# A second, shifted copy of exp(K) gives one of three small AV units its own PE row tiles

## The chip, the core and the metric

The kernel runs on one core of a Trainium2 chip. The metric is the device time of one execution in microseconds (us). Most executions of one kernel agree within 0.3%, so a gain of 1 us (0.3%) needs several rounds, or the trace, to be seen. Ratios are the mean time of one kernel's runs over that of the other's of the same rounds, so not quite the ratio of the medians that are quoted.

## The reference, cut to what matters

Local plus global attention (8 batches, 8 heads, 512 local and 32 global positions, head dimension 64), followed by a feed-forward block with a quick GELU. What the change touches is the part of the local queries that looks at the 32 global keys:

```python
s_lg = scale * np.matmul(q_l, k_g.transpose(0, 1, 3, 2))      # 512 x 32 for each head
s_l = np.concatenate([s_lg, s_ll], axis=-1)                   # beside the window of local keys
out_l = np.matmul(sm(s_l), np.concatenate([v_g, v_l], axis=2))
```

## The kernel before

Four heads make a "quad" and are worked on together; there are 16 quads. `K` computes the global-key scores of a quad into one PSUM bank (a section of the memory that matmuls write) `kb`, in two halves of the head dimension (`e` = 0, 1), each four matmuls with 32 rows and 32 columns of the PE array. `XK` takes the exponential: `ek`. `ekU` (the AV units of the title: attention weights times values) multiplies it with one of three stationary operands (unit 0: ones, for the sums; units 1 and 2: the two halves of the global values), and `U` adds the local keys to the same three banks with all 128 rows.

```python
def gk(self, out_, rhs, e=None):              # K(e): rows 32j, columns 32((j+1)%4)
    for ee in (0, 1) if e is None else (e,):
        for j in range(4):
            p = slice(32 * j, 32 * j + 32)
            r = 32 * ((j + 1) % 4)
            nc.tensor.matmul(out_[r : r + 32], lhsT=self.kg[p, :, ee], rhs=..., ...)

def ekU(self, unit, warm=0, ov=None):         # rows 32((j+1)%4), columns 32j, for every unit
    ...
    for j in range(4):
        r = 32 * ((j + 1) % 4)
        p = slice(r, r + 32)
        lv = (ones32[p] if unit == 0 else
              rvg[p, self.Q, :D].rearrange("p (w h) -> p w h", h=2)[:, :, unit - 1])
        nc.tensor.matmul(ov[32 * j : 32 * j + 32, :], lhsT=lv, rhs=self.ek[p], start=True, ...)

def ekUs(self, nxt=None, rnd=0, banks=(None, None, None)):
    if nxt:
        if rnd is not None:
            nxt.gg(rnd)                       # 8 matmuls of 32 columns, on K's tiles
        nxt.K(0)                              # the NEXT quad's scores, first half
    self.ekU(0, ov=banks[0])
    if nxt:
        nxt.K(1)                              # second half
    self.ekU(1, ov=banks[1])
    self.ekU(2, ov=banks[2])
```

In this kernel a matmul's rows of the array are those of its operands' partitions and its columns those of its output's partitions. All heads of `ek` stand at 32((j+1) mod 4), so all three units share four array tiles.

The softmax here doesn't subtract the row's maximum and nothing guards it: scores larger than these inputs give would overflow.

Of the kernel before, what the change touches and what calls it, by code (L numbers as in the profile page):

```python
# [13 lines left out]
BF16 = mybir.dt.bfloat16  # L14
# [6 lines left out]
def kernel(  # L21
# [12 lines left out]
    nc = tc.nc  # L34

    B, H, Sl, D = q_l.shape
# [8 lines left out]
    NQ = B * 2  # L45
# [9 lines left out]
    consts = ctx.enter_context(tc.tile_pool(name="consts", bufs=1))  # L55
    wts = ctx.enter_context(tc.tile_pool(name="wts", bufs=1))
    ld = ctx.enter_context(tc.tile_pool(name="ld", bufs=3))
    att = ctx.enter_context(tc.tile_pool(name="att", bufs=2))
# [14 lines left out]
    def load(b, us=(0, 1), kq=True):  # L73
        if b not in loaded:
            loaded[b] = (ld.tile([128, 2, 16 * D], BF16, name="rk"),
                         ld.tile([128, 2, 16 * D], BF16, name="rq"))
        if kq:
            s = slice(us[0], us[-1] + 1)
            nc.gpsimd.dma_start(out=loaded[b][1][:, s], in_=qf[b][:, s])
            nc.gpsimd.dma_start(out=loaded[b][0][:, s], in_=kf[b][:, s])  # L80
# [3 lines left out]
    def load_v(b, us=(0, 1)):  # L84
        s = slice(us[0], us[-1] + 1)
        hs = slice(4 * us[0], 4 * us[-1] + 4)
        for g in range(4):
            p = slice(32 * g, 32 * g + 32)
            nc.gpsimd.dma_start(out=vtiles[b % 2][p, s, :, :, :D], in_=vf[b, g][:, hs])  # L89
# [2 lines left out]
    rkg = consts.tile([128, NQ, D], BF16)  # L92

    rvg = consts.tile([128, NQ, D + 2], BF16)

    def load_turned(eng, out_, in_):
        eng.dma_start(out=out_[32:128], in_=in_[0:96])
        eng.dma_start(out=out_[0:32], in_=in_[96:128])

    def load_g(lo, hi):  # L100
        nc.gpsimd.dma_start(out=rkg[:, lo:hi, :], in_=kgf[:, lo:hi, :])
        nc.gpsimd.dma_start(out=rqg[:, lo:hi, :], in_=qgf[:, lo:hi, :])
        load_turned(nc.gpsimd, rvg[:, lo:hi, :D], vgf[:, lo:hi, :])
# [33 lines left out]
    for j in range(4):  # L137
        r = (j + 1) % 4
# [19 lines left out]
    def keep(n, ps, w=512):  # L158
        for _ in range(n):
            nc.tensor.matmul(ps[:, :w], lhsT=warm[:, 0:128], rhs=warm[:, :w], start=True, stop=True)  # L160
# [35 lines left out]
    def transpose_g(lo, hi, names="qk"):  # L196
        for name, dst, s in (("q", qgT, rqg), ("k", kgT, rkg)):
            if name not in names:
                continue
            nc.vector.transpose(dst[:, lo:hi, :32], s[:, lo:hi].bitcast(F32))  # L200
# [29 lines left out]
    def pbank(name):  # L230
        return psP.tile([128, 512], F32, name=name, tag="p")

    class Quad:
# [123 lines left out]
            self.gr = rnd  # L357
            self.gk((self.ps if rnd else self.spt(0))[:, 2, RW : RW + 32], self.qg)

        def XK(self):  # L360
            self.ek = att.tile([128, Sl], BF16, name="ek")
            nc.scalar.activation(self.ek, self.kb, AF.Exp, scale=scale)  # L362

        def ekU(self, unit, warm=0, ov=None):
            if ov is None:
                ov = pbank("ov")
            self.st[unit] = ov
            keep(warm, ov)
            for j in range(4):
                r = 32 * ((j + 1) % 4)  # L370
                p = slice(r, r + 32)
                lv = (ones32[p] if unit == 0 else
                      rvg[p, self.Q, :D].rearrange("p (w h) -> p w h", h=2)[:, :, unit - 1])
                nc.tensor.matmul(ov[32 * j : 32 * j + 32, :], lhsT=lv, rhs=self.ek[p],  # L374
                                 start=True, stop=False, skip_group_check=True)

        def ekUs(self, nxt=None, rnd=0, banks=(None, None, None)):
            if nxt:
                if rnd is not None:
                    nxt.gg(rnd)  # L380
                nxt.K(0)
            self.ekU(0, ov=banks[0])
            if nxt:
                nxt.K(1)
            self.ekU(1, ov=banks[1])
            self.ekU(2, ov=banks[2])

        def U(self, unit):
# [95 lines left out]
    def o_mm(i, st):  # L484
        tci, f4 = divmod(st, 4)
        first = (i, tci) not in ops
        if first:
            ops[i, tci] = pbank("op")
        op = ops[i, tci]
        for fc in range(4 * f4, 4 * f4 + 4):  # L490
            nc.tensor.matmul(op, lhsT=gTs[i][:, fc, tci * 128 : tci * 128 + 128],  # L491
                             rhs=w_out_sb[:, fc, :], start=(first and fc == 4 * f4), stop=(fc == FC - 1))
        if f4 == 3:
            o_out(i, tci, op)
# [27 lines left out]
    a, c = Quad(0), Quad(1)  # L522
# [35 lines left out]
    cast_g32("v", rvg)  # L558
    c.B(0)
    a.K()  # L560
    a.XK()
    c.S(0, added=True)
    c.gg()
    c.X(0)
    a.eg()
    c.K()
    c.XK()
    a.ekU(0)
    a.U(0)
    a.R()  # L570
# [51 lines left out]
    a, c = nq[1]  # L622
# [5 lines left out]
    a.gg()  # L628
    a.K()
    a.X(0)  # L630
    a.XK()
    a.M(0)
    a.eg()
    c.T()
# [10 lines left out]
    c.S(1)  # L645
    a.ekUs(c, 1)
    c.X(1)
    c.XK()
    for unit in range(3):
        a.U(unit)  # L650
    a.R()
# [20 lines left out]
    a, c = nq[2]  # L672
    load_v(3)
    load(4)
    load_g(8, NQ)
    gTs[1] = moe.tile([128, FC, TB], BF16, name="gT")
    hps = [pbank("hp") for _ in range(2)]
    for fc, kcs in ((0, (0, 1)), (1, (0, 1)), (0, (2, 3)), (1, (2, 3))):
# [20 lines left out]
    def phase_o(i):  # L699
        b = i + 1  # L700
        n = b + 1
        a, c = nq[b]
        if n < B:
            nq[n] = (Quad(2 * n), Quad(2 * n + 1))
            a2, c2 = nq[n]

        def o(tci):
            for f4 in range(4):
                o_mm(i, 4 * tci + f4)

        c.T()
        c.ext()
        a.S(1)
        a.X(1)
        a.M(1)
        o(0)
        c.S(0)
        a.UG(c)
        c.XK()
        c.X(0)  # L720
        a.RXG()
        c.M(0)
        c.eg()
        o(1)
        if n < B:
            a2.T()
            transpose_g(2 * n, 2 * n + 2)
            a2.ext()
        c.S(1)
        c.X(1)  # L730
        c.M(1)
        if n < B:
            o(2)
            a2.S(0)
            c.UG(a2)
            a2.XK()
            a2.X(0)
        else:
            for f4 in range(3):
                o_mm(i, 8 + f4)  # L740
            for unit in range(3):
                c.ekU(unit)
                c.U(unit)
            o_mm(i, 11)
            c.Gm()
        c.RXG()
        if n < B:
            a2.M(0)
            a2.eg()
        o(3)  # L750
        if i + 3 < B:
            load_v(i + 3)
        if i + 4 < B:
            load(i + 4)

    for i in range(1, B):
        if i > 1:
            for fc in range(FC):
                h_step(i, fc)
        if i + 1 < B:  # L760
            phase_o(i)
# [36 lines left out]
```

## Time and profile before

| | before |
|---|---|
| median (lowest to highest), first 3 runs | 311.05 us (310.76 to 311.09) |
| span of the profiled run | 309.3 us |
| PE busy, share of the span | 299.2 us, 97% |
| the stage from the first unit to the local products | 0.75 to 0.76 us, 11 times |

The prediction below shows the lines. PE is the matmul engine and PEld its weight loads; DVE, ACT and POOL are the vector, scalar and general engines; SP here only issues DMAs, as its queue SPq. The page gives busy times of each engine; "the chain that ended last" follows the last instruction back to what released it. In a timeline the columns are start, duration (both us), engine, line of the kernel, operation, output and inputs, shapes and count. Durations of matmuls overlap: what counts is when the next group starts.

### The profile page before, as it was taken

What the parts mean: (1) busy time and instruction counts of PE and PEld (TensorE: products, weight loads), DVE (VectorE), ACT (ScalarE), POOL (GpSimd) and SP (SyncE); (2) the same over time, 40 slices, a digit from 0 to 9 for tenths busy, and PEclk for the clock granted to TensorE, in tenths of its full rate; (3) what the DMA queues carried; (4) which work ended last, traced back from release to release, by engine and by line L of the source; (5) the groups of instructions that cost most, each with busy time, mean ns of one, the idle gap of its engine ahead of it and who ended that gap; (6) DMA issues with size and microseconds to landing.
All of it is one profiled execution on the core that took longest, in us unless ns stands there. A gap on an engine that the chain in (4) does not pass through costs nothing.

```text
span 309.3 us, 7765 instructions
## 1 busy us (share of the span) xinstructions
PE 299.2 (97%) x3230; PEld 149.3 (48%) x3265; DVE 211.0 (68%) x446; ACT 167.6 (54%) x251; POOL 54.1 (18%) x86
## 2 busy tenths in 40 slices
PE   7899999999999999999999999999999999999994
PEld 6544445444454455444454455445454454446653
DVE  6668857978957876776867876776777855573320
ACT  4728475475546735565556645565456651673421
POOL 8542754630050001400050002100000000000000
PEclk9999999999999999999999999999999999999999
DMA  7999999999289013951199013901120012201122
GB/s 193 176 209 206 201 138 217 213 184 100 61 79 192 5 36 72 131 107 30 45 95 173 8 37 71 101 0 36 36 61 10 2 44 46 51 0 35 35 68 69
DMA packets 53859, 27.60 MB, mean 89 GB/s; under 512 B 42432, under 2 KB 43712, under 8 KB 53824
## 3 DMA queue, kind: packets, MB, share of 16 engines
q0 software_dynamic: 45696, 16.95, 48.2%
q1 hardware_dynamic: 7648, 9.51, 12.6%
q10 hardware_dynamic: 480, 0.66, 0.7%
q8 instruction: 25, 0.41, 0.6%
q14 instruction: 10, 0.08, 0.1%
HBM read 35.13 MB, written 8.91 MB: 142 GB/s over the span
## 4 chain that ended last, share of the span: by engine, by line
PE 88%; DVE 4%; ACT 2%; DMA 2%; issue 1%; POOL 1%; ACTq 0%; POOLq 0%
PE op L491 35%; PE hp L466 35%; PE s L297 6%; PE ov L397 4%; PE ov L374 3%; DMA rk<-in_k_l_dram 2%; ACT e L327 1%; DVE xL L430 1%; PE s L316 1%; PE op L503 1%; DVE gT L474 1%; PE s L466 1%; PE s L415 1%; ACT th L473 1%; PE kb L316 1%
## 5 line engine op out<-in xcount | busy, mean ns | idle before, releaser
L491 PE MATMUL op<-w_out_sb,gT 128*128 128x512 bf16 x504 | 120.0, 380 | 1.7 <-issue 0.5
L474 DVE SCALAR_TENSOR_TENSOR gT<-th,hp 128x512 bf16<-128x512 f32 (+1 forms) x140 | 91.1, 656 | 41.8 <-ACT th L473 40.5
L466 PE MATMUL hp<-xL,w_in_sb 128*128 128x512 bf16 x487 | 108.4, 379 | 0.7
L473 ACT ACTIVATE th<-hp 128x512 f32<-128x512 f32 (+1 forms) x140 | 79.8, 573 | 42.9 <-PE hp L466 39.4
L466 PEld LDWEIGHTS <-w_in_sb 128*128 128x128 bf16 x576 | 56.1, 98 | 65.0 <-issue 1.3
L491 PEld LDWEIGHTS <-gT 128*128 128x128 bf16 x528 | 49.3, 98 | 56.4 <-issue 3.5
L327 ACT ACTIVATE e<-s 128x1712 bf16<-128x1712 f32 x31 | 49.5, 1597 | 15.8 <-PE s L415 8.9
L505 ACT ACTIVATE ob<-op 128x512 f32<-128x512 f32 (+2 forms) x35 | 20.5, 585 | 60.3 <-PE op L491 57.7
L89 POOL DMA_DIRECT2D v<-in_v_l_dram x24 | 18.7, 786 | 115.9 <-PE s L415 111.0
L421 DVE STREAM_TRANSPOSE sT<-ov 128x512 f32<-128x512 f32 x15 | 10.8, 717 | 29.1 <-PE ov L397 29.1
L334 DVE TENSOR_TENSOR e<-e,mask 128x1408 bf16<-128x1408 bf16 x28 | 24.4, 871 | 6.5 <-ACT e L327 6.5
L297 PE MATMUL s<-q,kT 32*128 32x228 bf16 (+5 forms) x528 | 21.1, 280 | 0.9 <-DVE q L259 0.7
L430 DVE TENSOR_TENSOR xL<-ov,rs 128x512 bf16<-128x512 f32 x30 | 19.4, 686 | 1.8 <-PE ov L397 0.5
L297 PEld LDWEIGHTS <-kT 32*128 32x128 bf16 x528 | 11.1, 95 | 14.8 <-issue 9.4
L255 DVE STREAM_TRANSPOSE kT<-rk 128x512 f32<-128x512 f32 (+1 forms) x17 | 16.9, 993 | 1.4 <-DMA rk<-in_k_l_dram 1.3
L362 ACT ACTIVATE ek<-kb 128x512 bf16<-128x512 f32 x16 | 9.6, 601 | 9.5 <-PE kb L316 9.5
L397 PE MATMUL ov<-e,v 128*32 128x160 bf16 (+1 forms) x480 | 12.1, 239 | 0.0
L425 DVE STREAM_TRANSPOSE rs<-rT 128x512 f32<-128x512 f32 x16 | 11.4, 711 | 0.5
L259 DVE STREAM_TRANSPOSE q<-rq 128x512 f32<-128x512 f32 (+1 forms) x17 | 10.7, 634 | 0.0
L397 PEld LDWEIGHTS <-v 128*32 128x32 bf16 x512 | 10.0, 97 | 0.9 <-issue 0.9
L316 PE MATMUL kb<-q,kgT 32*32 32x512 bf16 x128 | 10.0, 386 | 0.0
L466 PE MATMUL hp<-xG,w_in_sb 128*128 128x256 bf16 x64 | 9.6, 273 | 0.1
(78 smaller groups left out, 165.9 us busy)
## 6 DMA issues: line engine op xcount, KB each, us to landing
out_dram<-ob SPq DMA_DIRECT2D x132, 64.0 KB, 1.7
v<-in_v_l_dram POOLq DMA_DIRECT2D x32, 128.0 KB, 6.5
rq<-in_q_l_dram POOLq DMA_DIRECT2D x6, 512.0 KB, 8.5
rk<-in_k_l_dram POOLq DMA_DIRECT2D x6, 512.0 KB, 10.4
w_out_sb<-in_moe_w_out_dram POOLq DMA_DIRECT2D x4, 512.0 KB, 11.3
w_in_sb<-in_moe_w_in_dram POOLq DMA_DIRECT2D x4, 256.0 KB, 10.2
w_in_sb<-in_moe_w_in_dram POOLq DMA_DIRECT2D x2, 512.0 KB, 12.5
rq<-in_q_l_dram POOLq DMA_DIRECT2D x3, 256.0 KB, 7.9
```

The lines of the kernel that those rows point to most:

```text
L89: nc.gpsimd.dma_start(out=vtiles[b % 2][p, s, :, :, :D], in_=vf[b, g][:, hs])
L255: nc.vector.transpose(self.kT.rearrange("p (r t) -> p t r", t=16)[:, lo:hi], loaded[self.b][0][:, self.u].bitcast(F32)[:, 32 * lo : 32 * hi])
L297: nc.tensor.matmul(ps[j][:, off : off + n], lhsT=self.k[p, 128 * c : 128 * c + 128, e], rhs=self.q[p, lo:hi, r0 : r0 + nr, e], start=(e == ...
L327: nc.scalar.activation(e[:, :, :RW], self.ps[:, :, :RW], AF.Exp, scale=scale)
L334: nc.vector.tensor_mul(e, e, mask[:, rnd : rnd + 1, :].to_broadcast([128, 4, LW]))
L397: nc.tensor.matmul(ov[32 * j : 32 * j + 32, :].rearrange("p (t r) -> p t r", t=16)[:, :, r0 : r0 + nr], lhsT=lv, rhs=self.E[c // 2][:, j, ...
L430: nc.vector.tensor_mul(self.x[:, 2 * self.u + h, :], self.st[1 + h], self.st["rs"])
L466: nc.tensor.matmul(hp[:, : width(i)], lhsT=w_in_c[:, fc // 8, kc, fc % 8 // 2, :, fc % 2], rhs=(xL[i] if i < B else xG)[:, kc, :], start=( ...
L473: nc.scalar.activation(th[:, :n], hp[:, :n], AF.Tanh, scale=0.851)
L474: nc.vector.scalar_tensor_tensor(gTs[i][:, fc, :n], in0=th[:, :n], scalar=1.0, in1=hp[:, :n], op0=ALU.add, op1=ALU.mult)
L491: nc.tensor.matmul(op, lhsT=gTs[i][:, fc, tci * 128 : tci * 128 + 128], rhs=w_out_sb[:, fc, :], start=(first and fc == 4 * f4), stop=(fc = ...
L505: nc.scalar.activation(ob[:, lo:hi], op[:, lo:hi], AF.Copy, scale=0.5)
```

## The change

The intent: make a copy `ek2` of `ek` turned by 32 partitions, by DMA, and likewise of the global values (`rvt` from `rvg`); let unit 1 use the copies, so that it lands on other array tiles than unit 0 and the two run at once. Only quads 4 to 15 use it.

```diff
-        def XK(self):
+        def XK(self, two=True):
             self.ek = att.tile([128, Sl], BF16, name="ek")
             nc.scalar.activation(self.ek, self.kb, AF.Exp, scale=scale)
+            self.ek2 = None
+            if two:
+                self.ek2 = att.tile([128, Sl], BF16, name="ek2")
+                load_turned(nc.sync, self.ek2, self.ek)
...
             for j in range(4):
-                r = 32 * ((j + 1) % 4)
+                two = unit == 1 and self.ek2 is not None
+                r = 32 * ((j + 1 + two) % 4)
...
             self.ekU(0, ov=banks[0])
+            if self.ek2 is not None:
+                self.ekU(1, ov=banks[1])
             if nxt:
                 nxt.K(1)
-            self.ekU(1, ov=banks[1])
+            if self.ek2 is None:
+                self.ekU(1, ov=banks[1])
             self.ekU(2, ov=banks[2])
...
+    load_turned(nc.sync, rvt[:, 4:8], rvg[:, 4:8])
...
+        if i == 1:
+            load_turned(nc.sync, rvt[:, 8:NQ], rvg[:, 8:NQ])
```

(The operands follow: `rvt` and `ek2` in place of `rvg` and `ek` where `two` holds. The first four quads call `XK(False)`.)

More of the change, by code (lines that the diff above doesn't have):

```diff
@@ L94 @@
     rvg = consts.tile([128, NQ, D + 2], BF16)
+    rvt = consts.tile([128, NQ, D + 2], BF16)
     def load_turned(eng, out_, in_):
@@ L369, in ekU @@
             for j in range(4):
-                r = 32 * ((j + 1) % 4)
+                two = unit == 1 and self.ek2 is not None
+                r = 32 * ((j + 1 + two) % 4)
                 p = slice(r, r + 32)
                 lv = (ones32[p] if unit == 0 else
-                      rvg[p, self.Q, :D].rearrange("p (w h) -> p w h", h=2)[:, :, unit - 1])
-                nc.tensor.matmul(ov[32 * j : 32 * j + 32, :], lhsT=lv, rhs=self.ek[p],
+                      (rvt if two else rvg)[p, self.Q, :D].rearrange("p (w h) -> p w h", h=2)[:, :, unit - 1])
+                nc.tensor.matmul(ov[32 * j : 32 * j + 32, :], lhsT=lv, rhs=(self.ek2 if two else self.ek)[p],
                                  start=True, stop=False, skip_group_check=True)
@@ L560 @@
     a.K()
-    a.XK()
+    a.XK(False)
     c.S(0, added=True)
@@ L566 @@
     c.K()
-    c.XK()
+    c.XK(False)
     a.ekU(0)
@@ L630 @@
     a.X(0)
-    a.XK()
+    a.XK(False)
     a.M(0)
@@ L647 @@
     c.X(1)
-    c.XK()
+    c.XK(False)
     for unit in range(3):
```

## The prediction

> **What bounds the kernel now.** I read the page first (busy shares, clock, the chain that ended last), then the chain in order of time to find the stages that hold the touched instructions, then the PE timeline of one such stage, then ACT and the DMA beside it.
>
> ```profile
> PE 299.2 (97%) x3230; PEld 149.3 (48%) x3265; DVE 211.0 (68%) x446; ACT 167.6 (54%) x251; POOL 54.1 (18%) x86
> ...
> PEclk9999999999999999999999999999999999999999
> ...
> PE 88%; DVE 4%; ACT 2%; DMA 2%; issue 1%; POOL 1%; ACTq 0%; POOLq 0%
> ```
>
> TensorE is busy 97% of the span, at its full clock (0.998 granted), and 88% of the chain is PE; the next engine, DVE, has a third of its time free. So PE time taken away in the middle of the kernel should come off the end, unless a new wait eats it. From about 57 us on, the chain in order of time is almost purely PE. Its part round one changed stage:
>
> ```profile
> 150.75 3.56 PE op L491 x16
> 154.31 0.59 PE s L297 x16
> 155.05 0.23 PE ov L374 x4
> 155.70 1.03 PE ov L397 x47
> 156.90 0.32 PE op L491
> 157.27 3.18 PE op L491 x14
> ```
>
> L374 is the code that changes: the global-key AV products, three units of four 32x32 matmuls, each 512 columns wide. They lie between 16 score matmuls (L297) and the local AV products (L397). How they run is in the PE timeline:
>
> ```profile
> 154.90 0.40 PE L316 MATMUL kb<-q,kgT 32*32 32x512 bf16 x4
> 155.10 0.39 PE L374 MATMUL ov<-ek,rvg 32*32 32x512 bf16 x4
> 155.13 0.40 PE L316 MATMUL kb<-q,kgT 32*32 32x512 bf16 x4
> 155.32 0.38 PE L374 MATMUL ov<-ek,rvg 32*32 32x512 bf16 x4
> 155.63 0.49 PE L397 MATMUL ov<-e,ones 128*32 128x160 bf16 x16
> ```
>
> The reader sees waves. Unit 0 (the ones) starts at 154.88, unit 1 at 155.10, unit 2 at 155.32, the local products at 155.63. All three units use the same four PE tiles (32 rows at 32((j+1) mod 4), 32 columns at 32j), so they queue 0.22 us apart; four matmuls of one unit start within 11 ns of each other. The next head's global-key products (L316, kb) use the four tiles (j, j+1), and their halves run at 154.90 and 155.13, beside the units and not between them. So the stage is as long as the longest queue on one set of tiles: three waves for the units, two for kb. The last wave has to drain: from unit 2's start to the first local product it is 155.63 - 155.32 = 0.31 us, against 0.22 from wave to wave, so 0.09 us of drain.
>
> **What the Trainium skill says.** "TensorE: Matmul & The Clock Gate", Part 3: Packing small matmuls, says that tiles at different row and column groups run concurrently, starting about 4 ns apart, up to 16 tiles (10.6 times). The trace agrees for the 8 tiles of two sets: kb at 154.90 and unit 0 at 154.88 overlap, each 0.39 to 0.40 us long. No wave of this kernel has 12 tiles of 32x32 with 512 columns, which is what the change makes. "TensorEngine Tiling (Array Packing)", Key Properties, says that a change of tiling mode drains the TensorE; the 0.09 us agree, and the change doesn't remove it. "SBUF — State Buffer", A bandwidth-pool intuition that's wrong, gives the moving operand 128 lanes x 2 B x 2.4 GHz, one element per partition and cycle. If that were a hard limit, three streams out of one row group could not run at once. The trace contradicts it: 16 local products, of 128 rows and 160 or 192 columns (mean 176), start and are followed by the next 16 in 155.95 - 155.63 = 0.32 us; one stream at a time would take 16 x 176 / 2.4 GHz = 1.17 us. Some four streams per partition already run.
>
> **The change part by part.**
> Removed: unit 1 gets its own tiles (rows 32((j+2) mod 4), columns 32j), different from both other sets, and is issued straight after unit 0. The units' queue becomes two waves: units 0 and 1 at 154.88, unit 2 at 155.10. What ends last is now the second half of kb, still at 155.13, as it queues behind the first half on its own tiles. So the local products can start at 155.13 + 0.31 = 155.44 instead of 155.63: 0.19 us saved, not the 0.22 of a full wave.
> How often: a stage of this form occurs for each first quad of the phases 1 to 6 and each second quad of the phases 1 to 5, 11 in all. I looked at seven: unit 0 starts at 75.77, 86.07, 110.18, 144.58, 154.88, 178.99 and 247.80, and the local products 0.75 to 0.76 us later each time. The last quad issues unit by unit with local products in between, so its second copy gains nothing; the quads 0 to 3 keep the old order. Sum: 11 x 0.19 = 2.1 us.
> Added: 12 copies of a 128 KB tile from SBUF to SBUF, as two DMAs each on SP's queue, and four small copies for the turned values. None is on PE. The copy is issued when ek is done (146 us for the use at 154.9), and has to land before the next stage.
>
> ```profile
> 144.06 0.60 ACT L505 ACTIVATE ob<-op 128x512 f32<-128x512 f32 x1 [1.94 <-PE op L491]
> 145.28 0.60 ACT L362 ACTIVATE ek<-kb 128x512 bf16<-128x512 f32 x1 [0.63 <-PE kb L316]
> ```
>
> ek ends at 145.88. Between 145.9 and 154.9 stand 9 us. "DMA: Bandwidth & Descriptors", Anatomy of one DMA, gives some 2 us fixed per DMA; the trace's 64 KB output DMAs land 1.7 us after issue in the quiet stretch before 146 us and 6.6 us in the loads of 156 to 175 us. The copies made at 146 fall into the quiet stretch: two issues of 0.43 us (four output issues took 1.72 us), and some 2 us of landing, an estimate from these, make 3 us of the 9. Those made at 156.2 meet the loads, but are used only after an output stage and 16 hidden-layer steps, near 179 us, 22 us later. Both are hidden.
> Moved: unit 2 needs its bank 0.22 us earlier. In that stage it is the bank of the output tile copied by ACT at 144.06 to 144.66; unit 2 ran at 145.03 and now would at 144.81. That leaves 0.15 us, enough. Everything later is released by PE and moves with it: DVE's normalisation starts after the local sums and ends about 1 us before its reader, at the same distance as before.
> To pay: PE waits for one more semaphore (the DMA's) per stage. It is long satisfied; I take 0 to 0.03 us each, at most 0.3 us in sum, a guess as no such wait stands in this stage now. With 0.1 us of it, 311.05 - 2.1 + 0.1 = **309.0 us**, 0.65% faster.
>
> **The rivals.**
> 1. A third set doesn't overlap (rows, or PSUM columns, carry only two sets at once). Five sets of four at two at a time still take three waves: nothing gained, 311.0 us, or slightly worse. Against it: the score matmuls (32x128 at four row groups, all 16 sub-arrays) start four at a time, and the local products run four streams per partition. For it: the four score groups take 0.59 us for 16 x 214 columns, where four at a time at 2.4 GHz would be 0.36 us, so full occupation isn't free. A middle case, where 12 tiles run at 15% less speed, loses 0.03 us in the first wave: 309.4.
> 2. PE's instruction feed becomes the bound. From the scores to the end of the global products there are 112 pairs of weight load and matmul in 156.82 - 154.24 = 2.58 us, 23 ns a pair; the change asks for 21. The products after the waves already run at 68 pairs in 1.19 us, 17.5 ns a pair, though partly out of a queue filled before. Would cost up to the whole gain: 309.0 to 311.
> 3. The copy comes late, so the wait for a tile takes the place of the wait for a DMA. Where SP's queue stood behind an output DMA or the loads, a stage could lose microseconds. The times above speak against it; one late stage would make 310 to 312.
> 4. The extra DMA traffic (some 1.6 MB beside 27.6 MB) delays a load that somebody waits for. Before 77 us the queues are full, but only the first 10 us of the chain are DMA. Nothing, or 0.3 us.
>
> **Range and chances.** I give 75% to the main sum, with 1.7 to 2.4 us saved (308.7 to 309.4), 12% to a partial gain by rivals 1 or 2 (309.4 to 310.6), 8% to no gain (about 311), and 5% to a loss. The runs before lie within 0.33 us, so scatter adds little. Range for 8 in 10: **308.5 to 310.2**. 2% is 6.2 us; the gain can't reach it, since all L374 waves of these stages together are 11 x 0.75 = 8.3 us and two of three waves stay: 1% faster. A loss of 6.2 us would need every stage to wait half a microsecond for a copy: 2% slower. 97% within 2%.
>
> **What would show it right or wrong.** In the PE timeline of a changed stage: eight L374 matmuls (ones and unit 1) beginning within some 20 ns, beside the first kb half; unit 2 and the second kb half 0.22 us later; the local products 0.56 us after unit 0 instead of 0.75. PE's busy time falls by about 2 us. The copies land within 4 us in quiet stretches, and the list of waits has no PE wait on ek2. I would be wrong if unit 1 starts 0.1 us or more after unit 0, if 12-tile waves last clearly longer than 0.22 us, if a wait of PE on ek2 or rvt appears, or if the local products start sooner but the next output stage (L491) doesn't, which would be the feed.

## The result, and the profile after

| | before | after |
|---|---|---|
| median of 6 runs (lowest to highest) | 310.99 us (310.76 to 311.38) | 308.89 us (308.56 to 309.51) |
| ratio, 95% interval | | 0.9933 (0.992 to 0.9946) |
| span of the profiled run | 309.3 us | 307.3 us |
| PE busy | 299.2 us | 296.9 us |
| first unit to local products | 0.756 us | 0.582 us |

The gain is 2.1 us or 0.7%, clear of noise. The page of the kernel after, its busy line, its chain by engine and one of its DMA lines (output, input, queue, count, size of one, median us from issue to landing):

```profile
PE 296.9 (97%) x3230; PEld 148.9 (48%) x3265; DVE 211.0 (69%) x446; ACT 167.5 (55%) x251; POOL 54.4 (18%) x86
...
PE 90%; DVE 3%; DMA 2%; ACT 2%; issue 1%; POOL 1%; ACTq 0%; POOLq 0%
...
ek<-ek SPq DMA_DIRECT2D x12, 96.0 KB, 2.3
```

The same number of matmuls keeps PE busy for 2.3 us less, and PE still makes the chain. The PE timeline of the stage that was shown at 154.9 us (of the ones the first of four lines; the others lie within 10 ns):

```profile
154.10 0.39 PE L383 MATMUL ov<-ek,ones 32*32 32x512 bf16 x1
...
154.12 0.40 PE L383 MATMUL ov<-ek,rvt 32*32 32x512 bf16 x4
154.13 0.40 PE L319 MATMUL kb<-q,kgT 32*32 32x512 bf16 x4
154.33 0.39 PE L383 MATMUL ov<-ek,rvg 32*32 32x512 bf16 x4
154.36 0.39 PE L319 MATMUL kb<-q,kgT 32*32 32x512 bf16 x4
154.69 0.49 PE L409 MATMUL ov<-e,ones 128*32 128x160 bf16 x16
```

Unit 1 (`rvt`) now starts at 154.12, beside the ones (154.10) and the first half of kb, 12 tiles of 32x32 at once. Unit 2 follows at 154.33 and the second half of kb at 154.36. The local products start at 154.69, 0.58 us after the ones. The chain round it now has one piece of eight AV matmuls, the ones and unit 1, where before it had the four ones alone (the shorter pieces of the other units and of kb fall out of this view):

```profile
149.98 3.56 PE op L503 x16
153.54 0.59 PE s L300 x16
154.27 0.24 PE ov L383 x8
154.75 1.03 PE ov L409 x48
155.94 0.32 PE op L503
```

All 11 stages look alike (0.58 to 0.59 us). From the ones of the first of them to the ones of the last quad are 256.59 - 75.77 = 180.82 us before and 254.79 - 75.86 = 178.93 us after: 1.89 us, which is 11 x 0.172. The rest of the difference of the medians lies outside the changed stages and is not larger than the scatter of the runs.

### The profile page after: what moved, and what is told of

It reads as the page before. It is cut to its first block, busy times and chain, and to the rows that moved or that the text cites. A ratio compares the mean times of both kernels' runs of the same rounds, so it can differ in the third digit from the quotient of the medians.

```text
span 307.3 us, 7808 instructions
## 1 busy us (share of the span) xinstructions
PE 296.9 (97%) x3230; PEld 148.9 (48%) x3265; DVE 211.0 (69%) x446; ACT 167.5 (55%) x251; POOL 54.4 (18%) x86
## 4 chain that ended last, share of the span: by engine, by line
PE 90%; DVE 3%; DMA 2%; ACT 2%; issue 1%; POOL 1%; ACTq 0%; POOLq 0%
PE op L503 37%; PE hp L478 36%; PE s L300 6%; PE ov L409 4%; DMA rk<-in_k_l_dram 2%; PE ov L383 2%; ACT e L330 1%; DVE xL L442 1%; PE s L319 1%; PE op L515 1%; PE s L478 1%; PE s L427 1%; PE kb L319 0%; DVE sT L433 0%; DVE rs L437 0%
```

## The experiments

The theory: matmuls on different array tiles run side by side, those on one tile queue 0.22 us apart, and the stage is as long as the longest queue, plus the drain. The rivals: the gain comes from the new order or from the second buffer as such; the stage ends with the units and not with kb; the copies have a price. In the diffs, lines that only pass on operands are left out. "Time" is the median with the lowest and highest run; before on the same chips was 311.06 us for the first four and 311.05 us for the next four.

### The order alone

```diff
             self.ekU(0, ov=banks[0])
+            self.ekU(1, ov=banks[1])
             if nxt:
                 nxt.K(1)
-            self.ekU(1, ov=banks[1])
```

> The kernel before with only the new order: unit 1 issued ahead of the second half of kb, on its old tiles, with no second copy. Theory (queues on tiles): unit 1 still queues behind unit 0, so the ones start at 0, unit 1 at 0.23, the second kb half at 0.26, unit 2 at 0.44 and the local products at 0.756 us; time as before, 311.0 us (310.7 to 311.3). Rival (the order, not the tiles, made the gain): local products at 0.58 us and 308.9 us.

Measured: 310.90 us (310.82 to 311.38), ratio 0.9988 (0.9952 to 1.0023), local products at 0.756 us. Its PE timeline:

```profile
154.69 0.40 PE L316 MATMUL kb<-q,kgT 32*32 32x512 bf16 x4
154.89 0.38 PE L374 MATMUL ov<-ek,rvg 32*32 32x512 bf16 x4
154.92 0.40 PE L316 MATMUL kb<-q,kgT 32*32 32x512 bf16 x4
155.10 0.39 PE L374 MATMUL ov<-ek,rvg 32*32 32x512 bf16 x4
155.42 0.49 PE L397 MATMUL ov<-e,ones 128*32 128x160 bf16 x16
```

The three waves of before, to the hundredth. The order gives nothing by itself.

### The copies alone

```diff
-                two = unit == 1 and self.ek2 is not None
+                two = False
```

and the order of before. The copies are made, but no matmul reads them.

> The changed kernel with all its copies made but not used: the matmuls' order, operands and tiles are those of before. Theory (copies are hidden): 311.0 us (310.7 to 311.3), local products at 0.756 us after the ones, no new wait. Rival (the copies themselves cost time that the tiles' gain hides, or SP's queue delays outputs): 311.4 us or more.

Measured: 310.94 us (310.54 to 311.35), ratio 0.9985 (0.9953 to 1.0016), local products at 0.756 to 0.758 us. The copies cost nothing that can be seen. Why, the changed kernel's lines for `ek` show (durations of the issue in ns, minimum, median and maximum, then us to landing):

```profile
L100 SPq DMA_DIRECT2D ek<-ek x12: 527/527/2098, 53.4 to 248.1; - x12
...
DMA to landing us min/median/max: 1.9/2.3/7.3
```

Even the slowest copy lands in 7.3 us. In the changed kernel's trace each is used 8 us or more after `ek` is done, and had landed about 5 us or more before its reader started.

### The second copy on the wrong tiles

The copy is turned by 64 instead of 32 partitions, which puts unit 1 on the tiles of kb.

```diff
-                load_turned(nc.sync, self.ek2, self.ek)
+                load_half(nc.sync, self.ek2, self.ek)      # [64:128] <- [0:64], [0:64] <- [64:128]
...
-                r = 32 * ((j + 1 + two) % 4)
+                r = 32 * ((j + 1 + 2 * two) % 4)
```

> The changed kernel with the second copy shifted by 96 instead of 64 partitions against the heads' own rows, so that unit 1 lands on the four tiles that kb uses; order, copies and number of instructions stay. Theory (a tile's queue is what counts): unit 1 waits for the first kb half (start near 0.26), the second kb half starts near 0.49, the local products near 0.82 us, 0.06 us later than before the change in 11 stages: 311.6 us (311.2 to 312.1). Rival (any second copy will do, since it is the second operand buffer or the order that helps): 308.9 us.

Measured: 311.59 us (311.36 to 313.51), ratio 1.002 (0.9979 to 1.0061). The timeline of a stage whose ones start at 155.43:

```profile
155.45 0.40 PE L323 MATMUL kb<-q,kgT 32*32 32x512 bf16 x4
155.65 0.38 PE L387 MATMUL ov<-ek,rvg 32*32 32x512 bf16 x4
155.68 0.38 PE L387 MATMUL ov<-ek,rvt 32*32 32x512 bf16 x4
155.90 0.39 PE L323 MATMUL kb<-q,kgT 32*32 32x512 bf16 x4
156.22 0.49 PE L413 MATMUL ov<-e,ones 128*32 128x160 bf16 x16
```

As many matmuls and copies as in the change, in the same order, but unit 1 (`rvt`) stands in kb's queue: it starts at 0.25 us, after the first half of kb, and pushes the second half to 0.47. The local products come at 0.79 us, 0.03 us later than before the change (0.06 was expected, with the second half of kb at 0.49). Only the choice of tiles differs from the change, and it decides: the gain is gone, in the stage and in the time (the change's interval ends at 0.9946). That this kernel is slower than the one before is shown by the stage alone; the interval of the time holds 1.

### A third set of tiles

Unit 2 gets a third copy and the last free set (rows and columns 32j), and is issued ahead of the second half of kb.

```diff
+                self.ek3 = att.tile([128, Sl], BF16, name="ek3")
+                load_back(nc.sync, self.ek3, self.ek)      # turned by 32 the other way
...
-                r = 32 * ((j + 1 + two) % 4)
+                r = 32 * ((j + (1, 2, 0)[cp]) % 4)         # cp: 0, 1, 2 for the units 0, 1, 2
```

> The changed kernel plus a third copy, so that unit 2 gets the last free set of tiles (rows 32j, columns 32j) and is issued right after unit 1. Theory (the two kb halves, which queue on one set, now end the stage): the three units start within 0.04 us, the second kb half still at 0.27, the local products at 0.57 to 0.60 us: 308.9 us (308.5 to 309.3). Rival (the units still set the end): local products at 0.35 to 0.4 us, 306.6 us. A third reading, that 16 tiles at once run slower than 12, would show as a second kb half later than 0.27, and 309.1 to 310.

Measured: 309.08 us (308.84 to 310.87), ratio 0.9938 (0.9899 to 0.9978), local products at 0.58 us. A stage whose ones start at 119.87, and the ACT instruction before it:

```profile
119.88 0.40 PE L391 MATMUL ov<-ek,rvt 32*32 32x512 bf16 x4
119.89 0.40 PE L325 MATMUL kb<-q,kgT 32*32 32x512 bf16 x4
119.99 0.40 PE L391 MATMUL ov<-ek,rvb 32*32 32x512 bf16 x4
120.12 0.39 PE L325 MATMUL kb<-q,kgT 32*32 32x512 bf16 x4
120.45 0.49 PE L418 MATMUL ov<-e,ones 128*32 128x160 bf16 x16
```

```profile
119.34 0.60 ACT L526 ACTIVATE ob<-op 128x512 f32<-128x512 f32 x1 [1.94 <-PE op L512]
```

Nothing is gained: the second half of kb, on its own queue, ends the stage as in the change. Unit 2 starts at 0.12 us and not at 0.03 as I expected. ACT's copy out of unit 2's bank ends at 119.94, and unit 2 starts 0.05 us later; the matmul carries a wait for ACT. So there is a floor for unit 2 that no tile can lift, and the change, which starts it at 0.227, stays 0.1 us clear of it. With all 16 tiles in use from 0.12 us on, the second half of kb starts at 0.26 us as in the change: 16 tiles at once are not slower than 12 here.

### Without the second half of kb

Two kernels with a wrong sum (the scores miss half the head dimension; the comparison with the reference passes all the same, so a pass does not vouch for the global-key part): the change, and the third set, each without `nxt.K(1)` in the 11 stages.

```diff
-            if nxt:
+            if nxt and self.ek2 is None:
                 nxt.K(1)
```

> The changed kernel without the second half of kb in the 11 changed stages; the result is wrong on purpose (global-key scores of half the head dimension). Theory (the second kb half ends the stage; unit 2, 0.04 us ahead of it, comes next): local products at 0.541 us after the ones (0.227 + 0.314 of last wave and drain) instead of 0.582; 11 x 0.04 = 0.45 us less than the change, 308.4 us (308.1 to 308.8). Rival (the stage ends by the number of instructions, of which 8 of 56 go): local products at 0.50 us or earlier, 308.0 us or less. Rival (unit 2 alone sets the end): 0.582 us and 308.9 us.

> The third set of tiles of the earlier run and no second half of kb; the result is wrong on purpose. Theory (queues on tiles): nothing queues twice, so one wave is left; unit 2 starts at 0.122 us, when ACT has freed its bank, and the local products come at 0.122 + 0.314 = 0.44 us; 0.145 us less than the change in 11 stages: 307.3 us (306.9 to 307.7). Rival (16 tiles are no faster than 12 plus 4; the third set was idle gain): local products at 0.54 us or later, 308.4 us.

Measured: the change without it 308.60 us (308.30 to 308.85), ratio 0.9923 (0.9908 to 0.9938), local products at 0.541 us; the third set without it 307.73 us (307.61 to 308.05), ratio 0.9897 (0.9883 to 0.9911), local products at 0.447 us. First the change without it (ones at 119.99), then the third set without it (ones at 119.75):

```profile
120.22 0.38 PE L383 MATMUL ov<-ek,rvg 32*32 32x512 bf16 x4
120.53 0.49 PE L409 MATMUL ov<-e,ones 128*32 128x160 bf16 x16
```

```profile
119.76 0.40 PE L391 MATMUL ov<-ek,rvt 32*32 32x512 bf16 x4
119.78 0.40 PE L325 MATMUL kb<-q,kgT 32*32 32x512 bf16 x4
119.87 0.40 PE L391 MATMUL ov<-ek,rvb 32*32 32x512 bf16 x4
120.20 0.49 PE L418 MATMUL ov<-e,ones 128*32 128x160 bf16 x16
```

Both stages came out within 0.01 us of what was expected, so kb's second half is what ends the stage of the change; unit 2, which alone would end it 0.04 us sooner, comes next. The time of the second kernel is just above its range (307.7). Counted from the kernel before it fits: 11 x (0.756 - 0.447) = 3.4 us, measured 311.05 - 307.73 = 3.3. The two rivals, by number of instructions and by 16 tiles, fall: with all four sets and nothing queued twice one wave is left.

### The last quad, grouped

The change copies for the last quad too, but there the units alternate with the local products, which undoes it: its stage takes as long as before. This kernel groups them.

```diff
             for unit in range(3):
                 c.ekU(unit)
+            for unit in range(3):
                 c.U(unit)
             o_mm(i, 11)
             c.Gm()
```

> The changed kernel with the last quad's units grouped as in the other stages: the three global-key units first, then the three units of local products, instead of unit by unit (right result). The unit-by-unit stage takes 2.46 us from the ones to the next output matmul with five changes of tiling; grouped it has two waves and one change: 0.54 + 0.94 = 1.5 us. Theory (PE sets the end, DVE's normalisation has about 2 us of slack there): 0.96 us less than the change, 307.9 us (307.6 to 308.3). Rival (DVE's normalisation, which now starts 0.2 us later, or a bank, sets the pace): 308.9 us.

> The grouped last quad, and in that quad alone, where no kb competes, unit 2 on the third set of tiles (right result). Theory: one wave, local products at 0.34 instead of 0.54 us, 0.2 us less than the grouped kernel: 307.7 us (307.4 to 308.1), and the next output matmul at 1.28 us. Rival (the third set brings nothing, as in the stages with kb): as the grouped kernel, 307.9 us.

Measured: grouped 309.47 us (308.93 to 309.61), ratio 0.9948 (0.9936 to 0.9961); grouped with the third set in that quad 309.27 us (308.88 to 309.57), ratio 0.9945 (0.9933 to 0.9958). Both miss, by 1.6 us; what came is the rival that the first expectation named, DVE or a bank setting the pace. The PE timeline of the grouped kernel and its DVE timeline:

```profile
254.35 0.39 PE L383 MATMUL ov<-ek,ones 32*32 32x512 bf16 x4
254.89 0.49 PE L409 MATMUL ov<-e,ones 128*32 128x160 bf16 x16
255.93 1.04 PE L503 MATMUL op<-w_out_sb,gT 128*128 128x512 bf16 x4
256.89 0.32 PE L427 MATMUL og<-v,e 128*32 128x66 bf16 x16
258.04 3.61 PE L503 MATMUL op<-w_out_sb,gT 128*128 128x512 bf16 x16 [0.80 <-DVE xL L442]
```

```profile
255.44 0.72 DVE L433 STREAM_TRANSPOSE sT<-ov 128x512 f32<-128x512 f32 x1 [1.13 <-PE ov L409]
...
256.48 0.71 DVE L437 STREAM_TRANSPOSE rs<-rT 128x512 f32<-128x512 f32 x1
257.29 1.29 DVE L442 TENSOR_TENSOR xL<-ov,rs 128x512 bf16<-128x512 f32 x2
```

The stage itself did shrink: the output matmuls start 255.93 - 254.35 = 1.58 us after the ones. In the change it is 2.23 us, as its repeated run shows:

```profile
256.05 0.39 PE L383 MATMUL ov<-ek,ones 32*32 32x512 bf16 x4
...
258.28 1.04 PE L503 MATMUL op<-w_out_sb,gT 128*128 128x512 bf16 x4
```

(My 2.46 us was a misreading: in the first trace of the change, which I had used, only three of these four output matmuls are recorded, and I took the second for the first. So grouping has 0.65 us to give and not 0.96.) But then PE waits 0.80 us, for DVE's normalisation. The output tile does not read what DVE makes there; it waits for DVE to have read unit 1's bank, into which it is to write. DVE's chain starts when the sums are complete, which grouping delays by 0.2 us, so the output tile starts 258.04 - 254.35 = 3.69 us after the ones. In the first trace of the change, to which the next lines belong, it is 258.28 - 254.79 = 3.49:

```profile
254.79 0.39 PE L383 MATMUL ov<-ek,ones 32*32 32x512 bf16 x4
...
258.28 3.63 PE L503 MATMUL op<-w_out_sb,gT 128*128 128x512 bf16 x16
261.74 2.11 PE L478 MATMUL hp<-xL,w_in_sb 128*128 128x512 bf16 x9
```

I had counted the slack of DVE up to the reader of its result, the hidden layer, and overlooked the bank.

### The grouped quad with the wait taken away

To test that, the small global-query products (`Gm`) go behind the output tile. Banks are handed out in turn, so the output tile gets the bank that the sums leave first, which DVE has read after its first 0.7 us.

```diff
-            c.Gm()
-        c.RXG()
+        if n < B:
+            c.RXG()
+        else:
+            c.R(); c.XL(0); c.XL(1)
...
         o(3)
+        if n == B:
+            c.Gm(); c.G()
```

> The changed kernel once more, on the chip of the next two runs, as their baseline: 308.9 us (308.5 to 309.4), 2.1 us under the kernel before.

> The grouped last quad with its global-query products moved behind the last output tile of the phase, so that the output tile takes the bank that the sums free first and no longer the one that waits for DVE's normalisation (right result). Theory (in the grouped run PE stood 0.80 us before the output tile, waiting for that bank): the output tile starts 2.4 us after the ones instead of 3.5 (changed kernel), the hidden layer 0.8 us earlier: 308.1 us (307.7 to 308.5). Rival (grouping has nothing to give at this point, the DVE chain sets the pace anyway): 309.1 us, as measured for the grouped kernel.

> The same with unit 2 of the last quad on the third set of tiles (right result). Theory (with no kb there, a wave less counts, and nothing behind it waits for DVE now): 0.19 us less than the run without the third set, 307.9 us (307.5 to 308.3), local products at 0.353 us after the ones. Rival (its gain is lost again to a wait): no less than the run without it.

Measured on one chip, with before at 311.11 us (310.40 to 314.96):

| | median (lowest to highest) | ratio to before |
|---|---|---|
| the change again | 309.16 us (308.69 to 311.37) | 0.9941 (0.9893 to 0.9989) |
| grouped, `Gm` late | 308.40 us (308.11 to 308.59) | 0.9904 (0.9862 to 0.9946) |
| the same with the third set in the last quad | 308.36 us (308.21 to 309.14) | 0.991 (0.9867 to 0.9952) |

First the grouped kernel with `Gm` late, then the one with the third set (PE timelines):

```profile
254.47 0.39 PE L383 MATMUL ov<-ek,ones 32*32 32x512 bf16 x4
...
256.04 4.49 PE L503 MATMUL op<-w_out_sb,gT 128*128 128x512 bf16 x20
260.46 0.32 PE L427 MATMUL og<-v,e 128*32 128x66 bf16 x16
...
260.74 2.98 PE L478 MATMUL hp<-xL,w_in_sb 128*128 128x512 bf16 x13
```

```profile
254.66 0.39 PE L392 MATMUL ov<-ek,ones 32*32 32x512 bf16 x4
254.67 0.40 PE L392 MATMUL ov<-ek,rvt 32*32 32x512 bf16 x4
254.68 0.40 PE L392 MATMUL ov<-ek,rvb 32*32 32x512 bf16 x4
255.01 0.49 PE L418 MATMUL ov<-e,ones 128*32 128x160 bf16 x16
```

The wait is gone: 20 output matmuls run without a break. The hidden layer (hp) starts 260.74 - 254.47 = 6.27 us after the ones, against 261.74 - 254.79 = 6.95 in the change, so 0.7 us earlier: the whole 0.65 us that grouping takes off the stage (0.8 was expected). The measured time, 308.40, lies 0.8 us under the change on the same chip, and no run of one reaches into those of the other; but the intervals of their ratios overlap (two of the change's six runs had a clock of 0.99 and took over 310 us), so the 0.7 us of the trace are the better evidence. `Gm` late without the grouping was not run; in the change PE does not wait before that output tile, so nothing in its trace says that the move alone would gain. With the third set, where no kb competes, all three units start within 0.04 us, the local products follow at 0.35 instead of 0.54 us, and the hidden layer another 0.2 us earlier (6.08 us after the ones); its time cannot be told from the other's at this scatter. Both by their traces beat the kernel before and the change. The outputs are right.

## Why the prediction was right

- **The bound.** PE carries the chain before and after, and the time taken off PE in the stages came off the end.
- **Two waves instead of three, ended by kb.** Shown. Unit 1 starts at 0.014 us, the local products at 0.58; the run on kb's tiles and the order alone show that the tiles do it; the runs with and without the second half of kb show that kb ends the stage, and that a third set for unit 2 is no use there. (The kb products that run beside are the next quad's; "the next head's" in the prediction is a slip.)
- **0.19 us a stage.** Measured 0.174 in the stage shown, 0.172 in the mean of the 11. The term that was a little off is the last wave with its drain. I took 0.31 us from unit 2 and put it behind kb; from the second half of kb to the local products it is 154.69 - 154.36 = 0.33 us. The kernels on kb's tiles and with the third set, where kb ends the stage too, have 0.32 us there (156.22 - 155.90; 0.32 in the mean of the third set's 11 stages), and without the second half of kb it is again 0.31 from unit 2. Why the last wave is 0.01 to 0.02 us longer when it is kb's was not tested. 11 x 0.172 = 1.9 us instead of 2.1.
- **A price of 0.1 us for one more wait.** No such wait appears in the list of waits, and unit 1, which carries it, starts 0.014 us after the ones, on the heels of them. The guess offset about half of the 0.2 us that the line above promised too much. That 309.0 came so close to 308.89 is luck on top of a right mechanism: of the 2.1 us between the medians the stages account for 1.9, and the rest is within the scatter.
- **Copies hidden.** Shown by the kernel that only makes them. Their landing, 2.3 us in the median, is about what was estimated; their two issues take 0.53 and 0.59 us in the median instead of 0.43 each.
- **Unit 2's bank.** In the third set's kernel ACT's copy out of it ends 119.94 - 119.87 = 0.07 us after the ones, and the waiting unit 2 starts 0.05 us later, at 0.12; the change uses it at 0.227. The margin is 0.10 us; the 0.15 that was stated counts to the end of ACT's copy and leaves out the 0.05.
- **Rivals.** The third set of tiles does overlap, at 12 and at 16 tiles; instruction feed did not bind, since the local products still follow with the next 16 at 155.00 - 154.69 = 0.31 us; no copy was late. Of the added traffic no effect can be seen: the kernel that only makes the copies is no slower, and the loads of `v` land in 6.5 us in the median before, 7.4 in the change, and 6.3 in the kernel with `Gm` late, which makes the same copies.

My own proposal for the last quad failed at first for a reason that the prediction had worked out for the changed stages, and that I named as a rival for the new one but did not work out: who needs the bank next.

## What to carry to other kernels

Where small matmuls run on parts of the PE array, draw up the queue of each tile and shorten the longest one; here a copy by DMA made well ahead was a cheap way to another tile (no cost could be seen), and a tile that another queue uses was worse than none (0.79 us a stage instead of 0.76). As soon as one queue is shorter, name the next longest (here kb), because it sets the gain. And when work is moved earlier, follow not only the readers of each result but also the next writer of each bank that it occupies.

## What the Trainium skill lacked or had wrong

- "TensorE: Matmul & The Clock Gate", Part 3, The mechanism, says that matmuls start in program order ("strict FIFO, no reordering"). The starts that the profiler gives here are not: in the run on kb's tiles unit 2 (`rvg`) is last in the program, behind unit 1 and the second half of kb, and starts at 155.65, 0.03 and 0.25 us ahead of them. Each set of tiles keeps its own order. (The ends are modelled and say nothing on this.)
- "TensorEngine Tiling (Array Packing)", Gotcha 1: PSUM Pressure, says that different row tiles cannot access the same PSUM bank simultaneously. The four matmuls of one unit are on four different row tiles and write four quarters of one bank; they start within 11 ns of each other, and the next unit follows on the same tiles only 0.22 us later.
- "SBUF — State Buffer", A bandwidth-pool intuition that's wrong, gives the moving operand one element per partition and cycle. Three 32-row streams out of each row group run at once in the changed stages at 0.22 us per wave of 512 columns (3 x 512 / 0.22 us is some 7 elements per ns and partition, against 2.4), and four did, from 0.12 us on, in the kernel with the third set.
- No page says how long a change of the tiling drains: the last wave takes 0.31 us (0.32 to 0.33 when it is kb's) instead of 0.22 in these stages, 0.09 to 0.11 us more.
